# Attention chunks beside dense matmuls: one stretch per chunk, scores in quarters with the state's part, own part and update in halves

## The chip, the cores and the metric

One core of one Trainium2 chip. The metric is the device time of one execution in microseconds (us); lower is better. Stage times further down are read from a profiled execution's trace, whose span is some 2 us shorter than the device time of the same execution.

## The reference

A linear recurrence with a decay per head, for q, k, v of 4 x 8 heads x 768 steps x 64, followed by a two-layer network on its output, laid out as 3072 rows of 512.

```python
gamma = 1.0 - 2.0 ** (-5.0 - np.arange(H))
for t in range(S):                                  # S = 768, D = 64
    state = gamma * state + k[:, :, t] (outer) v[:, :, t]
    y[:, :, t] = q[:, :, t] @ state / sqrt(D)
x = y.transpose(0, 2, 1, 3).reshape(B * S, H * D)   # 3072 x 512
h = x @ w_in                                        # 512 x 2048
out = (h * sigmoid(1.702 * h)) @ w_out              # 2048 x 512
```

## The kernel before

The recurrence is computed by chunks of 128 steps: 24 chunks, six for each batch element. Matmuls run on TensorE and leave their results in PSUM tiles; SyncE's queue issues the input loads. The matmuls of the two-layer network are called dense below. A chunk goes through three steps.

- `turn`: q and k are transposed. For chunks 0 to 7 TensorE does it and ScalarE copies the result out of PSUM; for chunks 8 to 23 VectorE does it, in 32x32 squares, from tiles (`q_sq`, `k_sq`) that 16 small loads each have laid out for it.
- `attend`: the scores k·q of the chunk's eight heads into PSUM, then VectorE multiplies them with the mask of decays (`at`).
- `finish`: the part of the output that comes from the state of earlier chunks, the part from the chunk's own scores, the rescaling into X by VectorE, and the update of the state.

Four chunks make a block of 512 rows for the dense layers. Blocks 0 and 1 are multiplied plainly. From block 2 on, the up-projection takes seven products of half size in place of eight; every block's down-projection does. The steps of the next block's chunks are put between the 28 units (four matmuls, 1.73 us each) of a down-projection. So the time falls into a start-up (chunks 0 to 7 and the up-projection of block 0), the up-projection of block 1, and then for each block an output stage, with the next block's chunks in it where there are any, and the next up-projection.

```python
def turn(j, between=lambda: None):
    for name, store in (("q", QT), ("k", KT)):
        t = home(j, name + "T")
        if j < 2 * CB:                                   # CB = 4
            ...
            p = ps.tile([P, HP, P], F32, name="pt", tag="att")       # one bank, two buffers
            for hp in range(HP):
                pe.transpose(p[:, hp, :], ..., ident)
            act.activation(t, p, AF.Copy)
            between()
        else:
            tc.keep_in_program_order(dve.transpose(..., QKV.pop((name, j))...))
    ...
    if j % CB < 2 or j + 2 < 2 * CB:
        load(j + 2, "qk" if j + 2 < 2 * CB else "qkv")

def attend(j):
    p = ps_a.tile([P, 2, HP, P], F32, name="pa", tag="pa")           # two banks
    for hp in range(HP):
        for i in range(2):
            r = slice(i * D, (i + 1) * D)
            pe.matmul(p[:, i, hp, :], KT[j][r, hp, :], QT[j][r, hp, :], start=True, stop=True)
    AT[j] = home(j, "at")
    for i in range(2):
        dve.tensor_mul(AT[j][:, i], p[:, i], mask[:, i])

def finish(j):
    ...
    y = ps_a.tile([P, 2, HP, P], F32, name="py", tag="pa")           # the same two banks
    if c:                                                # state's part: 8 matmuls of 64x64
        for out, s, r in where: pe.matmul(out, old[k, s, :], qt[k, s, :], ...)
    for out, s, r in where:                              # own part: 8 of 128x64
        pe.matmul(out, vn[:, HP * r + s, :], a[:, r, s, :], ...)
    dve.tensor_mul(x[...], y[:, :, 0:2, :], rowd...)     # rescale
    ...
    u = ps.tile([P, HP, D], F32, name="pu", tag="att")   # update, in a tile of its own
    for s in range(HP):
        for r in range(2): pe.matmul(u[r * D:(r + 1) * D, s, :], kd[...], vn[...], ...)
    ...                                                  # new state = decay * old + u

# output stage of block m: one of the steps after every second unit
for n, unit in enumerate(down(m)):
    unit()
    ...
    if between and n % 2: between.pop(0)()
```

## Time and profile before

| | us |
|---|---|
| time, median of 3 runs | 713.88 (712.61 to 714.52) |
| start-up, up to the first dense matmul of 512 columns | 109.91 |
| output stage of block 1 (chunks 8 to 11 in it) | 62.61 |
| up-projection after it (no chunks) | 48.35 |
| output stages of blocks 2, 3, 4 | 62.49, 62.02, 62.62 |

In the rows of a timeline, the first two numbers are start and length in us, then the engine, the line of the program, the operation, output<-input, the tile shape of TensorE, the size of the moving operand and how many instructions the row groups. A bracket gives the idle time ahead and what ended it. L224, L245, L262, L264 and L278 are the transposes, scores, state's part, own part and update of the kernel before. Each matmul shows as two records (a transpose as one), so the 8 matmuls of the scores before are x16, the 16 quartered ones of the changed kernel x32. The granted clock is the share of its full speed at which TensorE ran.

The page's slices: busy tenths of TensorE and the granted clock in tenths, 40 slices of 17.8 us each.

```profile
PE   6799999999999999999999999999999999999997
PEclk9899999999999999999999999999999999999999
```

Apart from the last slice, TensorE has holes in the first two only, and the clock is low in the second only (0.8). TensorE's timeline of one turn in the start-up:

```profile
61.92 0.60 PE L224 MATMUL pt<-ident,q_in 128*128 128x128 f32 x4
62.36 0.60 PE L224 MATMUL pt<-ident,kn_in 128*128 128x128 f32 x4
```

The transposes of k follow those of q by 0.44 us, with no wait between. Each has a one-bank tile of its own.

### The profile page before, as it was taken

What the parts mean: (1) busy time and instruction counts of PE and PEld (TensorE: products, weight loads), DVE (VectorE), ACT (ScalarE), POOL (GpSimd) and SP (SyncE); (2) the same over time, 40 slices, a digit from 0 to 9 for tenths busy, and PEclk for the clock granted to TensorE, in tenths of its full rate; (3) what the DMA queues carried; (4) which work ended last, traced back from release to release, by engine and by line L of the source; (5) the groups of instructions that cost most, each with busy time, mean ns of one, the idle gap of its engine ahead of it and who ended that gap; (6) DMA issues with size and microseconds to landing.
All of it is one profiled execution on the core that took longest, in us unless ns stands there. A gap on an engine that the chain in (4) does not pass through costs nothing.

```text
span 710.8 us, 10300 instructions
## 1 busy us (share of the span) xinstructions
PE 692.4 (97%) x4109; PEld 572.5 (81%) x4109; DVE 363.7 (51%) x520; ACT 126.6 (18%) x197; POOL 111.5 (16%) x99
## 2 busy tenths in 40 slices
PE   6799999999999999999999999999999999999997
PEld 5688885447888888888888888888888888888886
DVE  4989889992612832443732443543345363344241
ACT  2322323311000001331000342000333000233000
POOL 2221010000564403000323000222000130200030
PEclk9899999999999999999999999999999999999999
DMA  9984443420012324101334200324300320000001
GB/s 228 290 213 116 135 147 119 135 35 8 15 46 41 74 46 104 35 0 20 74 60 102 46 0 11 75 47 88 66 1 3 72 45 24 23 1 1 15 1 44
DMA packets 143599, 46.31 MB, mean 65 GB/s; under 512 B 130752, under 2 KB 137408, under 8 KB 143552
## 3 DMA queue, kind: packets, MB, share of 16 engines
q1 hardware_dynamic: 134704, 38.84, 23.7%
q10 hardware_dynamic: 8848, 6.83, 3.1%
q8 instruction: 32, 0.52, 0.3%
q14 instruction: 15, 0.12, 0.1%
HBM read 39.33 MB, written 6.29 MB: 64 GB/s over the span
## 4 chain that ended last, share of the span: by engine, by line
PE 76%; DVE 12%; SPq 7%; issue 2%; DMA 2%; ACT 1%; DVEq 0%; ACTq 0%
PE pd L414 28%; PE px L363 16%; PE py L363 12%; PE ph L324 8%; SPq L132 6%; PE ph L311 6%; PE py L264 3%; DVE G L353 2%; PE pa L245 2%; PE py L262 2%; DVE G L354 1%; DVE G L248 1%; DVE G L352 1%; PE pu L278 1%; DMA k_sq<-in_k_dram 1%
## 5 line engine op out<-in xcount | busy, mean ns | idle before, releaser
L414 PE MATMUL pd<-W,G 128*128 128x256 f32 x1120 | 251.6, 382 | 0.4 <-DVE G L354 0.3
L414 PEld LDWEIGHTS pd<-W,G 128*128 128x128 f32 x1120 | 210.0, 190 | 31.7 <-DVE G L354 1.2
L363 PE MATMUL px<-X,W 128*128 128x256 f32 x512 | 119.0, 379 | 0.0
L363 PEld LDWEIGHTS px<-X,W 128*128 128x128 f32 x512 | 97.3, 190 | 13.2
L363 PE MATMUL py<-X,W 128*128 128x256 f32 x384 | 90.7, 379 | 0.0
L363 PEld LDWEIGHTS py<-X,W 128*128 128x128 f32 x384 | 73.0, 190 | 9.9
L311 PE MATMUL ph<-X,W 128*128 128x256 f32 x256 | 59.7, 388 | 0.0
L324 PE MATMUL ph<-W,W 128*128 128x512 f32 x128 | 55.1, 592 | 0.0
L311 PEld LDWEIGHTS ph<-X,W 128*128 128x128 f32 x256 | 48.3, 193 | 7.3 <-issue 0.2
L235 POOL TENSOR_TENSOR kd<-kn_in,cold 128x512 f32<-128x512 f32 x13 | 13.5, 1042 | 250.6 <-PE pu L278 202.0
L324 PEld LDWEIGHTS ph<-W,W 128*128 128x128 f32 x128 | 24.3, 190 | 30.2 <-issue 29.2
L355 POOL TENSOR_TENSOR G<-G 128x512 f32<-128x512 f32 x20 | 29.1, 1452 | 115.8 <-DVE G L354 113.6
L248 DVE TENSOR_TENSOR at<-pa,mask 128x512 f32<-128x512 f32 x32 | 20.6, 685 | 45.9 <-PE pa L245 45.9
L292 DVE TENSOR_TENSOR G<-G,sg 128x512 f32<-128x512 f32 x48 | 33.1, 689 | 13.7 <-ACT sg L290 13.7
L290 ACT ACTIVATE sg<-G 128x512 f32<-128x512 f32 x48 | 30.3, 631 | 51.3 <-DVE G L373 31.0
L290 ACT ACTIVATE sg<-ph 128x512 f32<-128x512 f32 x32 | 19.1, 597 | 102.3 <-PE ph L311 58.8
L414 PE MATMUL pd<-W,W 128*128 128x256 f32 x160 | 35.6, 380 | 0.4 <-DVE W L354 0.3
L414 PEld LDWEIGHTS pd<-W,W 128*128 128x128 f32 x160 | 30.2, 190 | 5.6 <-DVE W L354 1.2
L373 DVE TENSOR_TENSOR G<-py,p 128x512 f32<-128x512 f32 x16 | 11.1, 692 | 38.1 <-PE py L363 38.1
L401 ACT ACTIVATE u<-pd 128x512 f32<-128x512 f32 x6 | 3.6, 597 | 151.4 <-PE pd L414 151.4
L268 DVE TENSOR_TENSOR X<-py,rowd 128x512 f32<-128x512 f32 x20 | 13.7, 687 | 32.0 <-PE py L264 32.0
L387 DVE TENSOR_TENSOR G<-py,vv 128x512 f32<-128x512 f32 x16 | 11.1, 692 | 25.7 <-ACT vv L384 25.7
(97 smaller groups left out, 643.0 us busy)
## 6 DMA issues: line engine op xcount, KB each, us to landing
v_in<-in_v_dram SPq DMA_DIRECT2D x24, 256.0 KB, 3.9
W<-in_moe_w_in_dram SPq DMA_DIRECT2D x12, 512.0 KB, 5.2
out_dram<-o ACTq DMA_DIRECT2D x24, 256.0 KB, 2.8
W<-in_moe_w_out_dram SPq DMA_DIRECT2D x10, 512.0 KB, 3.7
q_sq<-in_q_dram SPq DMA_DIRECT2D x256, 16.0 KB, 1.8
k_sq<-in_k_dram SPq DMA_DIRECT2D x256, 16.0 KB, 1.7
kn_in<-in_k_dram SPq DMA_DIRECT2D x13, 256.0 KB, 3.3
G<-in_moe_w_out_dram SPq DMA_DIRECT2D x6, 512.0 KB, 3.6
```

The source lines that it names most:

```text
L132: tc.keep_in_program_order(sp.dma_start(t[r0:r0 + C4, hp], src[b, hp + HP * (r0 // D), rows, d0:d0 + C4].rearrange("(s p) d -> p s d", p=C4)))
L245: pe.matmul(p[:, i, hp, :], KT[j][r, hp, :], QT[j][r, hp, :], start=True, stop=True)
L248: dve.tensor_mul(AT[j][:, i], p[:, i], mask[:, i])
L262: pe.matmul(out, old[k, s, :], qt[k, s, :], start=(s < 2), stop=False, skip_group_check=True)
L264: pe.matmul(out, vn[:, HP * r + s, :], a[:, r, s, :], start=(not c and s < 2), stop=(s >= 2), skip_group_check=True)
L290: act.activation(s, h, AF.Sigmoid, scale=1.702)
L292: dve.tensor_mul(g, h[:, i], s[:, i])
L311: pe.matmul(h[:, ab], w, X[:, 2 * half + c // 2, c % 2, :], start=(ab == 0 and c == 0), stop=(c == 3), skip_group_check=True)
L324: pe.matmul(h, w, X1[:, c // 2:4:2, c % 2, :], start=(c == 0), stop=(c == 3))
L355: pool.tensor_sub(a[1], a[1], a[0])
L363: pe.matmul(acc[:, u, :], W1[:, 2 * d + u, sa, c, :], X[:, sb, c, :], start=(start and u == 0 and c == 0), stop=(stop and c == 1), skip_gr ...
L414: pe.matmul(p0[:, n, :], g1(m, p, sa)[:, n * P:(n + 1) * P], W2[:, sb, p, :], start=(new and p == 0 and n == 0), stop=(last and p == NP - ...
```

## The change

Each change of tile shape costs TensorE time (0.19 us, by the prediction's reading of the trace below). The intent is to let all of a chunk's small matmuls lie in one stretch between dense ones, with few changes of shape: the scores of chunk j+1, cut to 64x64 like the state's part of chunk j, then that state's part, then own part and update of chunk j, both of 128x64. Since the scores are a chunk ahead, the masks are ready when the own part comes. The scores and the output need separate PSUM tiles for that; the two banks come from the transposes and from the update, which move into the output's tile pair. For chunks 0 to 2 the output stays in the pair of the scores, now with the update in it. q's turned tile gets a second buffer, and loads and the decayed keys are issued later or earlier accordingly. The core of the diff:

```diff
@@ turn
-        for name, store in (("q", QT), ("k", KT)):
+        early = j < 2 * CB
+        if early:
+            p = ps_a.tile([P, 2, HP, P], F32, name="pt", tag="py")
+        for i, (name, store) in enumerate((("q", QT), ("k", KT))):
...
-                p = ps.tile([P, HP, P], F32, name="pt", tag="att")
                 for hp in range(HP):
-                    pe.transpose(p[:, hp, :], x[...], ident)
-                act.activation(t, p, AF.Copy)
+                    pe.transpose(p[:, i, hp, :], x[...], ident)
+                act.activation(t, p[:, i], AF.Copy)
                 between()
@@ attend
-    def attend(j):
+    def attend(j, f=None):
...
-            for i in range(2):
-                r = slice(i * D, (i + 1) * D)
-                pe.matmul(p[:, i, hp, :], KT[j][r, hp, :], QT[j][r, hp, :], start=True, stop=True)
+                for h in range(2):
+                    for i in range(2):
+                        r, t = slice(i * D, (i + 1) * D), slice(h * D, (h + 1) * D)
+                        pe.matmul(p[t, i, hp, :], kt[r, hp, t], qt[r, hp, :], start=True, stop=True)
+        if f is not None:
+            finish(f)
...
@@ finish
-        y = ps_a.tile([P, 2, HP, P], F32, name="py", tag="pa")
+        y = ps_a.tile([P, 2, HP, P], F32, name="py", tag="py" if j >= CB - 1 else "pa")
...
+        if c < NC - 1:
+            kd = KD.pop(j)
+            u = y[:, 0, 2:4, :]...                     # the update, in the output's tile
+            ... pe.matmul(u[...], kd[...], vn[...], start=False, ...)
         dve.tensor_mul(x[...], y[:, :, 0:2, :], rowd...)
...
-        u = ps.tile([P, HP, D], F32, name="pu", tag="att")
...
@@ order of the steps
-                for s in (lambda j=j: turn(j), lambda j=j: attend(j), lambda j=j: finish(j))]
+                for s in (lambda j=j: turn(j), lambda j=j: attend(j, j - 1))]
...
+        between, step = [], 3
+        if m == 1:
+            between = [lambda: turn(2 * CB), lambda: attend(2 * CB)] + chunks(2 * CB + 1, 3 * CB)
+            step = 2
...
-            if between and n % 2:
+            if between and n % step == step - 1:
                 between.pop(0)()
```

A step is taken after every third unit of an output stage, but after every second one in the stage of block 1, where five chunks are turned and scored in place of four (8 to 12).

More of the change, by code (lines that the diff above doesn't have):

```diff
@@ L125, in load @@
                 plain("kn", k, "k_sq", 2, True, sp if j else act)
-        else:
+        elif "q" in what:
             for name, src in (("q", q), ("k", k)):
@@ L135, in load @@
                 QKV[name, j] = t
-            if c < NC - 1:
+        if "v" in what:
+            if j >= 2 * CB and c < NC - 1:
                 plain("kn", k, "kn", 1)
-        if "v" in what:
             plain("v", v, "v", 2)
@@ L209, in home @@
         if j >= 2 * CB:
-            return one.tile([P] + shape, F32, name=name, tag=name)
+            return one.tile([P] + shape, F32, name=name, tag=name, bufs=2 - (at > 0))
         if at < 3:
@@ L216, in turn @@
     def turn(j, between=lambda: None):
-        for name, store in (("q", QT), ("k", KT)):
+        early = j < 2 * CB
+        if early:
+            p = ps_a.tile([P, 2, HP, P], F32, name="pt", tag="py")
+        for i, (name, store) in enumerate((("q", QT), ("k", KT))):
             t = home(j, name + "T")
-            if j < 2 * CB:
+            if early:
                 x = QKV["kn", j] if name == "k" else QKV.pop(("q", j))
-                p = ps.tile([P, HP, P], F32, name="pt", tag="att")
                 for hp in range(HP):
-                    pe.transpose(p[:, hp, :], x[:, 2 * hp:2 * hp + 2, :].rearrange("p i d -> p (i d)"), ident)
-                act.activation(t, p, AF.Copy)
+                    pe.transpose(p[:, i, hp, :], x[:, 2 * hp:2 * hp + 2, :].rearrange("p i d -> p (i d)"), ident)
+                act.activation(t, p[:, i], AF.Copy)
                 between()
@@ L230, in turn @@
             store[j] = t
-        if j % NC < NC - 1:
-            KD[j] = home(j, "kd")
-            x = QKV.pop(("kn", j)).rearrange("p h d -> p (h d)")
-            x = x.rearrange("p (s r d) -> p r s d", s=HP, r=2) if j < 2 * CB else x.rearrange("p (r s d) -> p r s d", r=2, s=HP)
-            pool.tensor_mul(KD[j].rearrange("p (r s) d -> p r s d", r=2), x,
-                            cold[:, H:2 * H].rearrange("p (r s) -> p r s", r=2)[:, :, :, None].to_broadcast([P, 2, HP, D]))
-        if j % CB < 2 or j + 2 < 2 * CB:
-            load(j + 2, "qk" if j + 2 < 2 * CB else "qkv")
@@ L240, in attend @@
-    def attend(j):
-        p = ps_a.tile([P, 2, HP, P], F32, name="pa", tag="pa")
-        for hp in range(HP):
-            for i in range(2):
-                r = slice(i * D, (i + 1) * D)
-                pe.matmul(p[:, i, hp, :], KT[j][r, hp, :], QT[j][r, hp, :], start=True, stop=True)
-        AT[j] = home(j, "at")
-        for i in range(2):
-            dve.tensor_mul(AT[j][:, i], p[:, i], mask[:, i])
-        KT.pop(j)
+        if early:
+            decay(j)
+        if j + 2 < NCH and (j + 2 < 2 * CB or not early):
+            load(j + 2, "qk")
@@ new lines, in decay @@
+    def decay(j):
+        if j % NC == NC - 1:
+            return
+        KD[j] = home(j, "kd")
+        x = QKV.pop(("kn", j)).rearrange("p h d -> p (h d)")
+        x = x.rearrange("p (s r d) -> p r s d", s=HP, r=2) if j < 2 * CB else x.rearrange("p (r s d) -> p r s d", r=2, s=HP)
+        pool.tensor_mul(KD[j].rearrange("p (r s) d -> p r s d", r=2), x,
+                        cold[:, H:2 * H].rearrange("p (r s) -> p r s", r=2)[:, :, :, None].to_broadcast([P, 2, HP, D]))
+    def attend(j, f=None):
+        if j is not None:
+            p = ps_a.tile([P, 2, HP, P], F32, name="pa", tag="pa")
+            kt, qt = KT.pop(j), QT[j]
+            for hp in range(HP):
+                for h in range(2):
[4 more added lines that the diff above has]
+            finish(f)
+        if j is not None:
+            AT[j] = home(j, "at")
+            for i in range(2):
+                dve.tensor_mul(AT[j][:, i], p[:, i], mask[:, i])
+            if j >= 2 * CB:
+                decay(j)
+        if f is not None and f + 2 < 2 * CB:
+            load(f + 2, "v")
+        if j is not None and 2 * CB <= j < NCH - 1:
+            load(j + 1, "v")
@@ L265, in finish @@
                       skip_group_check=True)
+        if c < NC - 1:
+            kd = KD.pop(j)
+            u = y[:, 0, 2:4, :].rearrange("p o t -> p (o t)").rearrange("p (s d) -> p s d", s=HP)
+            for s in range(HP):
+                for r in range(2):
+                    pe.matmul(u[r * D:(r + 1) * D, s, :], kd[:, HP * r + s, :], vn[:, HP * r + s, :],
+                              start=False, stop=True, skip_group_check=True)
         half, t0 = divmod(j % CB * P, TH)
@@ L269, in finish @@
                        rowd.rearrange("p (r o) t -> p r o t", r=2))
-        if j + 2 < 2 * CB:
-            load(j + 2, "v")
-        if c == NC - 1:
-            return
-        kd = KD.pop(j)
-        u = ps.tile([P, HP, D], F32, name="pu", tag="att")
-        for s in range(HP):
-            for r in range(2):
-                pe.matmul(u[r * D:(r + 1) * D, s, :], kd[:, HP * r + s, :], vn[:, HP * r + s, :],
-                          start=(s == 0), stop=True, skip_group_check=True)
         if c == 0:
             dve.tensor_copy(new, u)
-        else:
+        elif c < NC - 1:
             pool.tensor_mul(new, old, whole.rearrange("p a b -> p (a b)")[:, :, None].to_broadcast([P, HP, D]))
@@ L475, with chunks @@
                        pattern=[[0, H], [1, P]], channel_multiplier=-1)
-    def chunks(m):
-        return [s for j in range(m * CB, (m + 1) * CB)
-                for s in (lambda j=j: turn(j), lambda j=j: attend(j), lambda j=j: finish(j))]
+    def chunks(first, last):
+        return [s for j in range(first, last + 1)
+                for s in (lambda j=j: turn(j), lambda j=j: attend(j, j - 1))]
     keep_warm(7)
@@ L492 @@
                 fetch()
-        finish(j)
+        if j < CB - 1:
+            attend(None, j)
+        else:
+            attend(j + 1, j)
         if j == 0:
@@ L497 @@
             up0(0, j - 1)
-    between = chunks(1)[1:]
+    between = chunks(CB + 1, 2 * CB - 1) + [lambda: attend(None, 2 * CB - 1)]
     for n, unit in enumerate([(1, p) for p in range(3)] + [(half, p) for p in range(3, NP) for half in range(2)]):
@@ L502 @@
             narrow()
-        if between:
+        if between and n % 3 < 2:
             between.pop(0)()
@@ L511 @@
         if f >= NFF - 2:
-            load(2 * CB + f - NFF + 2)
+            load(2 * CB + f - NFF + 2, "qkv" if f == NFF - 2 else "qk")
     for m in range(NB):
-        between = chunks(m + 1) if 0 < m < NB - 1 else []
+        between, step = [], 3
+        if m == 1:
+            between = [lambda: turn(2 * CB), lambda: attend(2 * CB)] + chunks(2 * CB + 1, 3 * CB)
+            step = 2
+        elif 1 < m < NB - 2:
+            between = chunks((m + 1) * CB + 1, (m + 2) * CB)
+        elif m == NB - 2:
+            between = chunks((m + 1) * CB + 1, NCH - 1) + [lambda: attend(None, NCH - 1)]
         if m > 1:
@@ L517 @@
                 up(d)
-                if m + 1 < NB and d < 2:
-                    load((m + 1) * CB + d)
         for n, unit in enumerate(down(m)):
```

## The prediction

> **What bounds the kernel now.** I read the page's engine shares and chain first, then the order in time of TensorE, then that of the input queue. The share line and the chain of the page:
>
> ```profile
> PE 692.4 (97%) x4109; PEld 572.5 (81%) x4109; DVE 363.7 (51%) x520; ACT 126.6 (18%) x197; POOL 111.5 (16%) x99
> PE 76%; DVE 12%; SPq 7%; issue 2%; DMA 2%; ACT 1%; DVEq 0%; ACTq 0%
> ```
>
> TensorE is busy nearly all of the span and 76% of the chain; but 7% of the chain is the SyncE queue that issues the loads (SPq) and 2% its transfers. So a saving on TensorE counts in full only while that queue keeps ahead. One attention chunk of the stage that writes output block 1 (the start, the length and the group of each row of TensorE's timeline; the bracket is idle time and its releaser):
>
> ```profile
> 242.20 7.17 PE L414 MATMUL pd<-W,G 128*128 128x256 f32 x32
> 249.30 1.16 PE L245 MATMUL pa<-qT,kT 64*128 64x128 f32 x16
> 250.40 3.72 PE L414 MATMUL pd<-W,G 128*128 128x256 f32 x16
> 254.05 0.67 PE L262 MATMUL py<-qT,state 64*64 64x128 f32 x16
> 254.64 1.15 PE L264 MATMUL py<-at,v_in 128*64 128x128 f32 x16
> 255.57 0.69 PE L278 MATMUL pu<-v_in,kd 128*64 128x64 f32 x16
> 256.18 7.17 PE L414 MATMUL pd<-W,G 128*128 128x256 f32 x32
> ```
>
> A chunk is cut in two by dense work: scores (L245), 16 dense records, then state part (L262), own part (L264), update (L278). Use start to start, not the modelled ends. Dense records alone come every 216 ns (64 of them take 13.81 us, 200.28 to 214.10). The chunk lasts 256.18 - 242.20 = 13.98 us, of which 48 dense records are 48 x 0.216 = 10.36; attention therefore costs 3.62 us of TensorE, with no wait in it. Record by record inside a group, a pair of 64-row tiles comes every 112 ns, a set of four 64x64 tiles every 109 ns, a pair of 64-column tiles every 109 ns, and every 58.5 ns with 64 moving columns. Eight pairs, four sets of four, eight pairs, eight pairs: 0.89 + 0.44 + 0.87 + 0.47 = 2.67 us. The other 0.95 us are the five changes of tile shape, 0.19 each.
>
> **What the Trainium skill says.** "TensorEngine Tiling (Array Packing)", Key Properties: "Changing tiling mode (not just tile) drains the TensorE". The trace agrees: the last score record starts at 221.987, the next dense one 0.20 us later, and the one after it 0.32 later instead of 0.216. "TensorE: Matmul & The Clock Gate", Part 3, says that tiles of different row and column groups run together; the four-at-once sets above show it (109 ns for four, 109 for two). The same page, Part 1, says that an idle TensorE is throttled to half its clock until it has been busy for some 3.4 us. The trace has it in the beginning: behind a wait of 2.81 us
>
> ```profile
> 20.81 0.67 PE L262 MATMUL py<-G,state 64*64 64x128 f32 x16 [2.81 <-DVE G L248]
> 23.55 4.73 PE L311 MATMUL ph<-X,W 128*128 128x256 f32 x16
> ```
>
> 16 dense records last a microsecond longer than the 3.65 that they usually take, and the granted clock is 0.79 from 24 to 36 us. "DMA: Bandwidth & Descriptors", Issuing engines are not separate DMA queues, calls the sequencer's time to initiate a DMA "usually small relative to the DMA itself". Here it is not: q and k of a chunk take 32 issues of 0.43 us at a pace of 0.474, one behind the other, while the 16 DMA engines are only 24% to 37% busy; the issuing is what binds.
>
> **The change, part by part.**
>
> (a) Shape changes. Scores of chunk j+1 become 16 matmuls of 64x64 (32 records) right ahead of chunk j's state part, which has the same shape; own part and update are of one shape already. A stretch is now dense, quarters, halves, dense: three changes for five. Work: 8 + 4 sets of four at 109 ns = 1.31, 0.87 own, 0.47 update, together 2.65 us, against 2.67: quartering the scores gains nothing itself. With 3 x 0.19 = 0.57 a full stretch costs 3.2 us, so 0.41 less per chunk.
>
> (b) Waits on the masks. Scores used to be masked by VectorE just ahead of the own part; TensorE waited for it 0.17 to 0.25 us once per block and 0.43 and 0.45 in the start-up. Now a whole step lies between. The second PSUM tile pair (py), paid for by the two banks that transposes and update had, also lets scores start without waiting for the previous output's reading. Gain about 0.25 per block, 1 us in the start-up.
>
> (c) Start-up. Until about 45 us VectorE is 95% busy narrowing weights and sets the pace; nothing is won there, and the scores of chunk 1 now wait for the update's copy as well (some 1 us lost). Chunks 4 to 7 win 4 x 0.41 plus 1 us of waits: net -1.5.
>
> (d) Sum over stages without new waits. Block 1's output stage has one more score stretch (chunk 12's) than before: 62.6 us becomes 48.4 dense + 0.1 + 1.25 (scores of chunk 8 alone) + 3 x 3.2 + 2.75 = 62.1: -0.5. The next two: four stretches each, -1.45 and -1.4. The fourth has three full ones and a last one without scores (1.9): 62.6 to 60.0, -2.6. With -1.5: **-7.5 us**, 706.4.
>
> (e) The loads. This is where I expect the loss. The stage of block 1 now does a step after every two units of 1.73 us, and runs through five chunks' scores, not four. A chunk is due every 4 x 1.73 + 3.2 = 10.1 us (before, 14.0). The queue:
>
> ```profile
> 215.63 7.51 SPq L132 DMA_DIRECT2D q_sq<-in_q_dram  x16
> 223.24 9.10 SPq L132 DMA_DIRECT2D k_sq<-in_k_dram  x16
> 232.45 0.39 SPq L120 DMA_DIRECT2D kn_in<-in_k_dram  x1
> 232.94 0.53 SPq L120 DMA_DIRECT2D v_in<-in_v_dram  x1
> 233.56 9.66 SPq L132 DMA_DIRECT2D q_sq<-in_q_dram  x16
> 243.32 7.49 SPq L132 DMA_DIRECT2D k_sq<-in_k_dram  x16
> 250.90 0.38 SPq L120 DMA_DIRECT2D v_in<-in_v_dram  x1
> 251.39 8.83 SPq L132 DMA_DIRECT2D q_sq<-in_q_dram  x16
> 260.32 7.49 SPq L132 DMA_DIRECT2D k_sq<-in_k_dram  x16
> ```
>
> One chunk occupies it for 233.56 - 215.63 = 17.9 us, just to issue. Only chunks 8 and 9 are in before the stage; 10 can start when VectorE has turned chunk 8 over and freed its buffer:
>
> ```profile
> 214.91 0.70 DVE L228 STREAM_TRANSPOSE qT<-q_sq 128x512 f32<-128x512 f32 x1
> 215.53 0.67 DVE L228 STREAM_TRANSPOSE kT<-k_sq 128x512 f32<-128x512 f32 x1
> ```
>
> that is 1.5 us after the stage's start at 214.1. VectorE's order in the changed kernel has these two in the same place behind the last addition of block 0, so the start is the same. Loads of chunks 10, 11 and 12 then take 267.8 - 215.6 = 52.2 us, less 0.5 for a v that comes later now. q and k of chunk 12 have been issued 53.2 us into the stage, land 1.75 us later and are turned over in 2 x 0.65: ready at 56.3. TensorE wants them behind 20 units of 1.73, 1.3 for chunk 8's scores and three stretches: 34.5 + 0.1 + 1.3 + 9.6 = 45.5. **TensorE loses about 10.8 us there**, some 2.5 of it already at chunk 11 (issued at 35, ready at 38, wanted at 35.4) and the rest at chunk 12. v of chunk 10 and decayed keys (1.04 us of GpSimd) come just behind and add little. An idle time of eight microseconds also lowers the clock: +1.5, an estimate from the 1.0 and the slower small matmuls after the 2.81 us wait.
>
> Later stages hold: a chunk is due every 13.6 us against 17.9, but two are loaded ahead during the up-projection (48.4 us without chunks), so only two must arrive during a stage, at about 21 and 39 us, and they are wanted at 37 and 51. The keys of the next block's first chunk land about 58 us in; the sums of X that stand behind them in GpSimd's order are needed at about 65. No loss, with some 4 us to spare.
>
> Sum: 713.9 - 7.5 + 10.8 + 1.5 = 718.7.
>
> **The rivals.**
> 1. No starvation. If the queue got its start earlier, or issued at its bare rate (0.474 us each, 15.2 for 32), chunk 12 would be ready near 51 and 6 us would be lost; with none at all the result is 706. For it: every one of the queue's longer pauses (1.3 to 1.8 us) may depend on other traffic. Against: three chunks in a row took 17.9 us in this very stage, and the second and third blocks show 16.4 to 18.1.
> 2. More starvation: GpSimd's sums stand behind keys that come late in the third or fourth stage and stall the next up-projection: 2 to 5 us each, to 723. For it: the orders do put those keys between the sums. Against: the margins above.
> 3. The shape changes don't become cheaper, since the drain depends on what follows rather than on their number: then 7.5 falls to about 3, and the result is near 722.
> 4. VectorE's start-up chain shifts by one or two microseconds, either way.
>
> **Range and chances.** I centre a little below the sum, at 717, since rival 1 lies far to one side. 8 in 10: 706 (hardly any starvation) to 723 (rival 2 or 3). Faster by 2% needs 699.6, below even the case without new waits: 0.02. Slower by 2% needs 728: 0.04.
>
> **What would show it.** (a) Right if a full stretch takes 3.1 to 3.3 us beyond its dense records; wrong at 3.5 and more. (b) Right if no wait on the masked scores is left after 50 us. (e) Right if TensorE has an idle time of 5 to 9 us ahead of scores in block 1's stage, released by VectorE's turning of k, which itself waited for a k load; the queue would be unbroken through that stage. The other three stages should be 1.4 to 2.6 us shorter than before. The prediction is wrong if that idle time is missing, or if a wait of that size appears ahead of an up-projection.

## The result

| | before | changed |
|---|---|---|
| time, median of 4 runs | 714.2 (712.61 to 714.88) | 722.84 (721.8 to 724.79) |
| mean clock, profiled run | 0.995 | 0.986 |
| span, profiled run | 710.8 | 721.3 |

The ratio is 1.0127, with a 95% interval of 1.0099 to 1.0155: the changed kernel is slower by 1.3%, less than the 2% of the classes but clear of the noise. A ratio here is the mean time of one kernel's fast runs over that of the other's of the same rounds, so not quite the ratio of the medians.

By stages of the two traces:

| stage | before | changed | difference | expected |
|---|---|---|---|---|
| start-up | 109.91 | 117.17 | +7.26 | -1.5 |
| output of block 1 | 62.61 | 72.06 | +9.45 | +11.8 (-0.5 + 10.8 + 1.5) |
| up-projection after it | 48.35 | 48.35 | 0 | 0 |
| output of block 2 | 62.49 | 60.74 | -1.75 | -1.45 |
| output of block 3 | 62.02 | 60.27 | -1.75 | -1.4 |
| output of block 4 | 62.62 | 59.84 | -2.78 | -2.6 |
| sum | | | +10.4 | +4.9 |

The sum agrees with the spans (721.3 - 710.8 = 10.5). One expectation in this table has the wrong sign, the first.

The page after: engine shares, the chain's shares, and the slices (18.0 us each).

```profile
PE 689.9 (96%) x4493; PEld 574.2 (80%) x4493; DVE 360.3 (50%) x520; ACT 127.3 (18%) x197; POOL 110.8 (15%) x99
PE 86%; DVE 6%; SPq 3%; ACT 2%; DMA 2%; issue 1%; DVEq 0%; ACTq 0%
...
PE   5889899999999987999999999999999999999997
PEclk9699999999999998999999999999999999999999
```

TensorE is busy 2.5 us less than before although it has 384 more instructions. The holes are at two places: in the first three slices and the fifth, and in the 15th and 16th (252 to 288 us). The clock drops to 0.6 in the second slice and to 0.8 in the 16th. The chain's share of the input queue has become smaller, 3% after 7%, so the average says nothing of the queue's harm, which lies in one stage. An ordinary stretch, in the stage of block 2 (L258, L283, L285 and L293 are scores, state's part, own part and update):

```profile
354.79 10.63 PE L433 MATMUL pd<-W,G 128*128 128x256 f32 x48
365.34 1.10 PE L258 MATMUL pa<-qT,kT 64*64 64x128 f32 x32
366.27 0.62 PE L283 MATMUL py<-qT,state 64*64 64x128 f32 x16
366.81 1.14 PE L285 MATMUL py<-at,v_in 128*64 128x128 f32 x16
367.74 0.68 PE L293 MATMUL py<-v_in,kd 128*64 128x64 f32 x16
368.35 10.63 PE L433 MATMUL pd<-W,G 128*128 128x256 f32 x48
```

From 354.79 to 368.35 are 13.56 us; 48 dense records take 48 x 0.216 = 10.36; the stretch costs 3.20, where before the same work cost 3.62. No bracket is left. This part is as intended. The stage of block 1 isn't; TensorE's timeline there, from the scores of chunk 10 on:

```profile
248.03 1.10 PE L258 MATMUL pa<-qT,kT 64*64 64x128 f32 x32 [1.36 <-DVE kT L230]
...
275.38 1.98 PE L258 MATMUL pa<-qT,kT 64*64 64x128 f32 x32 [6.56 <-DVE kT L230]
277.11 1.10 PE L283 MATMUL py<-qT,state 64*64 64x128 f32 x16
278.14 1.42 PE L285 MATMUL py<-at,v_in 128*64 128x128 f32 x16
279.50 14.08 PE L433 MATMUL pd<-W,G 128*128 128x256 f32 x64
```

The scores of chunk 10 wait 1.36 us; a row left out, the own part of chunk 10, waits 0.42 us for the load of v. The scores of chunk 12 wait 6.56 us for VectorE's turning of k. Behind the wait the small matmuls are slow: scores 277.11 - 275.38 = 1.73 us in place of 0.92, state's part 1.03 in place of 0.54, own part 1.36 in place of 1.07; together 1.6 us. The granted clock was 0.50 from 272 to 278 us. VectorE's row ahead of it, and the input queue's issues of that stage:

```profile
274.52 0.71 DVE L230 STREAM_TRANSPOSE kT<-k_sq 128x512 f32<-128x512 f32 x1 [4.90 <-DMA k_sq<-in_k_dram]
```

```profile
222.89 8.67 SPq L132 DMA_DIRECT2D q_sq<-in_q_dram  x16
231.66 7.73 SPq L132 DMA_DIRECT2D k_sq<-in_k_dram  x16
...
265.55 7.49 SPq L132 DMA_DIRECT2D k_sq<-in_k_dram  x16
```

Between these rows the queue is never idle for more than a tenth of a microsecond: three chunks take 273.04 - 222.89 = 50.2 us just to issue. VectorE waits for its loads, TensorE for VectorE.

What had not been foreseen is in the start-up. The turn of chunk 5, and the row of the transposes in the view of waits (engine, line, releaser: us in total, times, longest):

```profile
57.06 0.60 PE L226 MATMUL pt<-ident,q_in 128*128 128x128 f32 x4
59.41 0.66 PE L226 MATMUL pt<-ident,kn_in 128*128 128x128 f32 x4 [1.75 <-ACT G L227]
```

```profile
PE pt L226 <- ACT G L227: 9.9, 8, 2.7
```

The transposes of k now wait for ScalarE in each of the eight early chunks, 9.9 us in all. L227 is the copy of q's transposes out of PSUM. Before, there was no wait on ScalarE ahead of a transpose. (The 22.1 us in the first expectation below add the weight loads' waits for the same copies, 12.2 us; that is largely the same time counted twice.) VectorE, which the prediction took to set the pace here, was busy for 29.0 of the first 45 us, after 33.5 before the change.

### The profile page after: what moved, and what is told of

It reads as the page before. It is cut to its first block, busy times and chain, and to the rows that moved or that the text cites. A ratio compares the mean times of both kernels' runs of the same rounds, so it can differ in the third digit from the quotient of the medians.

```text
span 721.3 us, 11040 instructions
## 1 busy us (share of the span) xinstructions
PE 689.9 (96%) x4493; PEld 574.2 (80%) x4493; DVE 360.3 (50%) x520; ACT 127.3 (18%) x197; POOL 110.8 (15%) x99
## 4 chain that ended last, share of the span: by engine, by line
PE 86%; DVE 6%; SPq 3%; ACT 2%; DMA 2%; issue 1%; DVEq 0%; ACTq 0%
PE pd L433 35%; PE px L382 15%; PE py L382 11%; PE ph L343 8%; PE ph L330 7%; SPq L132 3%; PE py L285 3%; PE pa L258 3%; PE py L283 1%; PE py L293 1%; ACT W L188 1%; PE pt L226 1%; ACT G L227 1%; DVE W L372 1%; DVE G L372 1%
## 5 line engine op out<-in xcount | busy, mean ns | idle before, releaser
L433 PE MATMUL pd<-W,G 128*128 128x256 f32 x1120 | 247.6, 381 | 0.4 <-DVE G L373 0.3
L258 PE MATMUL pa<-qT,kT 64*64 64x128 f32 x512 | 18.5, 285 | 7.9 <-DVE kT L230 7.9
L424 DVE TENSOR_TENSOR o<-pd,vv 128x512 f32<-128x512 f32 x12 | 7.7, 686 | 35.9 <-ACT vv L420 35.9
```

Of the source, the lines that this page charges most:

```text
L258: pe.matmul(p[t, i, hp, :], kt[r, hp, t], qt[r, hp, :], start=True, stop=True)
L433: pe.matmul(p0[:, n, :], g1(m, p, sa)[:, n * P:(n + 1) * P], W2[:, sb, p, :], start=(new and p == 0 and n == 0), stop=(last and p == NP - ...
```

## The experiments

Three theories stood for the start-up: (T) the transposes of q and k share one PSUM tile, so those of k wait until q's half has been copied; (U) the update lies in the output's tile, so the rescaling waits for the update's matmuls and, in chunks 0 to 2, the next scores, which use the same pair, wait for the copy of the state; (V) nothing of both: VectorE's chain of narrowing weights shifted, or it is chance. For the stage of block 1: (Q) one queue's issuing is too slow for five chunks; (B) the transfers themselves are; (P) only the pace of the steps matters.

The start-up depends on chance as well, so each kernel's start-up time is split at the first run of 32 dense records. The part behind it repeats within 0.05 us for one kernel.

### The kernels as they are, once more

The kernel before twice, the changed one once, unedited, to learn how much a start-up varies.

> The kernel before, once more with a profile, to see how far chance moves its start-up: 109.9 us in the one profile so far; 109 to 112 expected. All later stages as before to 0.2 us.

> The kernel before a third time, for the same reason: start-up 109 to 112 us, all later stages as before to 0.2 us.

> The changed kernel once more with a profile: start-up 115.5 to 119.5 us, as in its own profile (117.2) and the two variants that share its start-up (119.4 and 115.4); block 1's stage 71.5 to 73.

| | time, us | start-up | of it behind the first 32 dense | stage of block 1 |
|---|---|---|---|---|
| before (first trace) | 712.85 | 109.91 | 65.53 | 62.61 |
| before_again | 713.96 | 111.06 | 65.54 | 62.62 |
| before_third | 712.94 | 109.57 | 65.53 | 62.62 |
| changed (first trace) | 723.16 | 117.17 | 67.12 | 72.06 |
| after_again | 722.29 | 115.85 | 67.12 | 72.07 |

The stage of block 1 and the second part of the start-up repeat; the first part moves by 1.5 us in these traces. The runs e3 and e5 below, whose start-up code is that of the changed kernel, reach the split at 52.26 and 48.26 us, so its first part moves by 4.0. The clock goes with it: up to the split the mean granted clock was 0.86 and 0.87 in the changed kernel's first trace (split at 50.05) and e3, and 0.93 in after_again (48.73) and e5. Still, the kernel before needs 109.6 to 111.1 us and the changed start-up 115.4 to 119.4 in all its traces, so chance (V) is not the account of the loss. In the changed kernel the scores of chunk 4 lie ahead of the split and in the kernel before behind it, 1.1 us in the trace; a comparison between these two kinds has to allow for that.

### e1_own_banks: a PSUM tile for each of q and k

```diff
-            p = ps_a.tile([P, 2, HP, P], F32, name="pt", tag="py")
...
+                p = ps.tile([P, HP, P], F32, name="pt", tag="xy"[i])
-                    pe.transpose(p[:, i, hp, :], x[...], ident)
-                act.activation(t, p[:, i], AF.Copy)
+                    pe.transpose(p[:, hp, :], x[...], ident)
+                act.activation(t, p, AF.Copy)
```

> The changed kernel, with the transposes of q and of k in two tiles of one PSUM bank each (taken from the banks of the up-projection's outputs) and not in the two halves of one tile. Theory A (k's transposes of a chunk wait until ScalarE has read q's, since both stand in one tile; the 22.1 us of waits for ScalarE's copy in the changed kernel's start-up come from this): those waits go, the start-up (first dense matmul of 512 columns at 117.2 us; before the change 109.9) comes to 110 to 112, and the time falls from 722.8 to 716 to 718. Rival B (the start-up is lost since scores wait for the state update that now stands in the output's tile, and by VectorE's order): the waits move there, start-up stays at 115 to 117, time 721 to 723.

Measured: 720.02 us, ratio to before 1.0085 (1.0062 to 1.0107). Start-up 113.35, of it behind the split 63.51 in place of 67.12. The time was expected at 716 to 718 and the start-up at 110 to 112; the gain was smaller. The turn of chunk 5, and the dense row behind the turn of chunk 6:

```profile
56.85 0.60 PE L225 MATMUL pt<-ident,q_in 128*128 128x128 f32 x4
57.29 0.60 PE L225 MATMUL pt<-ident,kn_in 128*128 128x128 f32 x4
...
73.10 3.72 PE L329 MATMUL ph<-X,W 128*128 128x256 f32 x16 [0.77 <-DVE W L310]
```

k follows q by 0.44 us again, as before the change. The waits that went away behind the split are 1.75, 0.79 and 1.80 us (chunks 5, 6 and 7 of the changed kernel), 4.3 together; 0.77 came back as a wait for VectorE, and 3.6 remain. That supports T, with a size. Ahead of the split no transpose waits for ScalarE either, but the scores of chunks 0 and 4 then do (2.42 and 0.81 us), and this part is no shorter than the scatter allows (49.84). The stage of block 1, where no such transposes are, took 73.06 us here, and 73.0 to 73.1 in e2 and e6 as well, in place of 72.06. In e1 the microsecond lies in the waits for loads: 7.08 in place of 6.56 at chunk 12 and 0.75 in place of 0.42 for v, with a slower own part behind them.

### e2_one_copy: one shared tile, but one copy after all eight transposes

```diff
-                act.activation(t, p[:, i], AF.Copy)
-                between()
+                if i:
+                    both = G[:, 0:2, j % 2 * 2:j % 2 * 2 + 2].rearrange("p a s t -> p a (s t)")
+                    act.activation(both, p.rearrange("p a b c -> p a (b c)"), AF.Copy)
+                    between()
+                    between()
```

> The changed kernel with its one tile for both transposes kept, but one ScalarE copy for both halves behind all eight transposes, so that none of them waits for a copy. Theory A: as with two tiles, start-up at 110 to 113, since a copy of 1024 columns takes some 1.1 us and only the first five chunks' scores wait for it directly; time 716 to 719. Rival B: no change, 721 to 723.

Measured: 716.92 us, ratio 1.0039 (1.0016 to 1.0062). Start-up 112.58, behind the split 62.59 (a wait of 0.19 us cuts the first run of 32 in two here; its start is taken). The turn of chunk 5:

```profile
57.46 0.60 PE L226 MATMUL pt<-ident,q_in 128*128 128x128 f32 x4
57.90 0.60 PE L226 MATMUL pt<-ident,kn_in 128*128 128x128 f32 x4
```

The tile is still shared and no second tile is used; only the reading between q and k is gone, and with it the loss. So the number and place of the banks didn't cost the time; what did is that TensorE had to wait with one half of a tile until ScalarE had read the other. In time it is 3.1 us ahead of e1; 0.9 of that is behind the split in the profile. The rest was not followed up: the profiled run of e2 is the slowest of its four (719.63), and e1's first part of the start-up (49.84 and 49.99 for e2) gives none of it.

### e3_pace: the ten steps of block 1's stage spread over 26 units, not 20

```diff
-            if between and n % step == step - 1:
+            if between and (n in (1, 3, 6, 9, 11, 14, 17, 20, 23, 25) if m == 1 else n % step == step - 1):
```

> The changed kernel with the ten attention steps of block 1's output stage spread over 26 of its 28 units and not over 20, so that each chunk is wanted after its loads. Theory C (that stage waits for the load queue, which needs 17 us a chunk to issue): its length falls from 72.1 us to 62 to 63.5, the 6.6 us of idle time ahead of chunk 12's scores goes to under 0.7, and the time falls by 8.5 to 10 to 713 to 714.5. Rival D (the loads would come later too, since each load is issued behind the step that frees its buffer): the idle time stays above 3 us, time 717 to 722. The sums of X then stand closer to the next up-projection, which must show no wait for them.

Measured: 715.57 us, ratio 1.003 (1.0004 to 1.0055); the stage of block 1 took 62.70 us in place of 72.06. Start-up 119.40, with the shared tile still there (67.14 behind the split). The scores of chunk 12:

```profile
280.18 1.10 PE L258 MATMUL pa<-qT,kT 64*64 64x128 f32 x32
```

They start without any wait; those of chunk 10 still wait 0.69 us, and the up-projection behind gets a new wait, 1.10 us for a copy by ScalarE (e9 shows the like). That stage took 49.68 in place of 48.35. With the slower pace the wait for loads at chunk 12 is gone, but this doesn't tell Q from B: both have more time.

### e4_banks_pace: e1 and e3 together

The edit is that of e1 and that of e3.

> Both edits together. If A and C are both right and independent, the gains add: 722.8 - 5 to 7 - 8.5 to 10 = 706 to 709, which beats the kernel before by some 1%. If only C is right, 713 to 714; if the start-up's gain is lost in a later wait, 712 or more.

Measured: 709.86 us, ratio 0.995 (0.9932 to 0.9969), start-up 111.32, stage of block 1 62.71, up-projection behind it 49.53. Each stage shows the gain of its own repair. Both repairs together are worth 722.84 - 709.86 = 13.0 us, where alone they gave 2.8 and 7.3; the 2.9 us above the sum were not taken apart, but the traces differ in two more places: e1's longer waits for loads (1.0) are gone, and the first part of the start-up took 47.81 us after 49.84 in e1, at a mean granted clock of 0.93 after 0.86. The result is faster than the kernel before.

### e5_k_on_act: ScalarE's queue issues the k loads of chunks 10 to 12

```diff
-                        tc.keep_in_program_order(sp.dma_start(
+                        tc.keep_in_program_order((act if name == "k" and CB * 2 + 2 <= j <= CB * 3 else sp).dma_start(
```

> The changed kernel with its fast pace kept, but the k loads of chunks 10, 11 and 12 issued on ScalarE's queue beside the q loads on SyncE's. Same bytes, same pieces, same DMA engines. Theory C1 (the stage of block 1 is bound by the time one queue takes to issue, 0.474 us each): chunk 12 is ready before it is wanted, the stage falls from 72.1 us to 62 to 64, time 713 to 715. Rival D1 (bound by the DMA engines or the memory, not by issuing): the two queues share the same engines, each load lands later, the stage stays above 68 us, time 719 or more.

Measured: 713.75 us, ratio 0.9999 (0.9977 to 1.0021). The pace is that of the changed kernel, the bytes are the same; the stage of block 1 took 63.38 us. TensorE's scores of chunks 10 and 12, then the issues of both queues:

```profile
246.25 1.10 PE L258 MATMUL pa<-qT,kT 64*64 64x128 f32 x32 [1.37 <-DVE kT L230]
...
266.48 1.10 PE L258 MATMUL pa<-qT,kT 64*64 64x128 f32 x32
```

```profile
221.10 18.33 SPq L132 DMA_DIRECT2D q_sq<-in_q_dram  x32
...
245.54 8.54 SPq L132 DMA_DIRECT2D q_sq<-in_q_dram  x16
```

```profile
221.74 9.36 ACTq L132 DMA_DIRECT2D k_sq<-in_k_dram  x16
231.38 8.41 ACTq L132 DMA_DIRECT2D k_sq<-in_k_dram  x16
```

q and k of a chunk are issued side by side, and the queues now have pauses: none issues a load from 241.4 to 245.5 us. The waits at chunk 12 and for v are gone, and so are 8.7 us of this stage; the up-projection behind took 48.88 in place of 48.35, with a wait of 0.29 us for ScalarE's copy. This decides between Q and B in favour of Q: the same transfers, issued by two queues, are in time. It also speaks against P as the whole account, since the pace is unchanged. The 1.37 us at chunk 10 stayed although its loads came in half the time, so that part isn't the queue's: VectorE turns chunk 10 over directly behind six additions (239.7 to 244.8 us), with no wait for a load.

### e6_u_apart: e1, and for chunks 0 to 2 the rescaling first and the update in a tile of its own

```diff
(the edit of e1, and:)
+        def rescale(): ...                             # the tensor_mul into X, as before
+        if j < CB - 1:
+            rescale()
+            kd = KD.pop(j)
+            u = ps.tile([P, HP, D], F32, name="pu", tag="xy"[j % 2])
+            for s in range(HP):
+                for r in range(2):
+                    pe.matmul(u[r * D:(r + 1) * D, s, :], kd[:, HP * r + s, :], vn[:, HP * r + s, :],
+                              start=(s == 0), stop=True, skip_group_check=True)
+        elif c < NC - 1:
...
-        dve.tensor_mul(x[...], y[:, :, 0:2, :], rowd...)
+        if j >= CB - 1:
+            rescale()
```

> The run with transposes in two banks (start-up 113.4 us, time 720.0), and besides the update of the state of chunks 0 to 2 in a bank of its own again, behind the rescaling of the output as before the change. Theory B (what is left of the start-up's loss, 3.4 us in that run, comes from the update standing in the output's tile: the rescaling waits for the update's matmuls, the next scores for VectorE's copy of the state, and TensorE's clock falls in these waits): the first dense matmuls of 256 columns begin at 23.5 to 24.5 us and not at 29.0, the start-up comes to 107.5 to 109.5 (before the change 109.9), time 714 to 716.5. Rival: the loss is VectorE's order alone or chance in the first loads; the start-up stays at 112 or more, time 718 to 721.

Measured: 717.24 us, ratio 1.0045 (1.002 to 1.0071), start-up 111.12, behind the split 63.51 as e1; 107.5 to 109.5 and 714 to 716.5 were expected. The scores of chunk 1 in TensorE's timeline of e6:

```profile
16.22 1.10 PE L257 MATMUL pa<-G 64*64 64x128 f32 x32 [0.41 <-DVE X L289]
```

In the changed kernel these scores wait 1.81 us, released by VectorE's copy of the state; here 0.41, released by the rescaling. The first dense matmuls start at 25.70 (before 23.55, changed 28.56). All three kernels with the update apart have start-ups of 110.0 to 111.1, mean 110.6, the two with only the tiles separated (e1, e4) 113.35 and 111.32, mean 112.3. So U is worth about 1.7 us. That is within the scatter of one start-up; it is the difference of means, and the wait in the trace, that carry it. So do the first dense matmuls: they start between 24.36 and 25.70 us in these three kernels, and between 27.57 and 30.53 in the seven traces with the update in the output's tile. Part of the 1.7 us is a low clock: e1 has a mean of 0.86 up to the split, and at the same 0.93 the split comes at 47.81 us in e4 and at 47.08 and 46.49 in e8 and e9.

### e7_quarters_alone: the kernel before, with only the scores quartered

```diff
-            for i in range(2):
-                r = slice(i * D, (i + 1) * D)
-                pe.matmul(p[:, i, hp, :], KT[j][r, hp, :], QT[j][r, hp, :], start=True, stop=True)
+            for h in range(2):
+                for i in range(2):
+                    r, t = slice(i * D, (i + 1) * D), slice(h * D, (h + 1) * D)
+                    pe.matmul(p[t, i, hp, :], KT[j][r, hp, t], QT[j][r, hp, :], start=True, stop=True)
```

> The kernel before the change with nothing but its scores cut into quarters of 64x64 (16 matmuls for 8). The prediction said that this gains nothing itself: scores stay at 1.09 us a chunk, time within 0.5 of 713.9. The changed kernel's trace has them at 1.03 where they stand alone, so the rival is a gain of 0.06 x 24 = 1.4 us: 712.5.

Measured: 713.75 us, ratio 0.9996 (0.9972 to 1.002): no change in time. In the trace the scores with their change of shape take 1.034 us in place of 1.092, and the four stages with chunks are 0.17 to 0.18 us shorter each, while the start-up behind the split takes 0.34 longer (65.87). The time can't separate no gain from the rival's 1.4 us. Twice as many instructions of half the size neither cost nor win anything that a time would show. The gain of the stretches is that of their order.

### e8_apart_act: e6 and e5 together

The edit is that of e6 and that of e5.

> All three: transposes in two banks, early updates apart, k loads of chunks 10 to 12 on ScalarE's queue. If the three causes are independent: start-up 107.5 to 109.5, block 1's stage 62 to 64, time 704.5 to 707, which is faster than the kernel before by some 1.1%; above 710 would mean that one gain is lost in another wait.

Measured: 709.31 us, ratio 0.9943 (0.9915 to 0.997). Start-up 110.59, stage of block 1 63.38, up-projection 48.35. All three causes are taken away, and the mean clock is 0.995 again. The expectation, 704.5 to 707 with a start-up of 107.5 to 109.5, was missed: the stage of block 1 came as expected, the start-up didn't, and what (c) hoped to win there is not seen.

### e9_best: e8, with block 1's steps a unit later from the scores of chunk 10 on

```diff
-            if between and n % step == step - 1:
+            if between and (n in (1, 3, 5, 7, 9, 12, 14, 16, 18, 20) if m == 1 else n % step == step - 1):
```

> The best of the runs so far (transposes in two banks, early updates apart, k loads of chunks 10 to 12 also on ScalarE's queue), with the steps of block 1's output stage one unit later from chunk 10's scores on. In the run without this the stage took 63.4 us, with 1.43 us of waiting ahead of chunk 10's scores, since VectorE turns chunk 10 over behind six additions that wait for TensorE. Expected: that wait goes, the stage takes 61.9 to 62.2 us, the start-up 110 to 112, time 707 to 709. If the wait only moves along, 63 us and 709 to 710.

Measured in five rounds: 707.91 us (705.92 to 710.01) against 714.5 of the kernel before; ratio 0.9909 (0.9888 to 0.993). It beats both kernels. The stage of block 1 took 61.94 us, without a wait; the wait at chunk 10 was one of pace, and is gone: VectorE's turn of chunk 10, behind the same six additions, is now done before TensorE wants it. The up-projection behind took 50.39 in place of 48.35. Its first rows on TensorE, ScalarE's output stores of that time and ScalarE's copy:

```profile
281.57 1.97 PE L393 MATMUL px<-X,W 128*128 128x256 f32 x8 [1.80 <-ACT p L400]
```

```profile
274.11 6.62 ACTq L436 DMA_DIRECT2D out_dram<-o  x3
280.83 0.60 ACT L400 ACTIVATE p<-px 128x512 f32<-128x512 f32 x1 [10.73 <-DMA k_sq<-in_k_dram]
```

ScalarE's sequencer is occupied with issuing three stores until 280.73, and does its copy directly behind. TensorE waits 1.80 us for that copy. (The bracket of the copy names a load, but the copy comes 0.1 us behind the last issue.) So in its trace e9 gives back 2.04 where it wins 1.44 in block 1's stage, and the intervals of e8 and e9 overlap: that e9 is ahead of e8 isn't shown, only that both are ahead of the kernel before. A wait for the same copy was there in e3.

## Why the prediction was right or wrong

The time fell into the range, at its upper end: 722.84 for 706 to 723. That was luck: the upper end was kept for rivals 2 and 3, neither of which came, and the loss that carried the time there, the start-up's, stood in no rival at this size. The change itself was told badly: +3.1 expected (717 against 713.9), +8.6 measured.

- **(a), shape changes: right.** A full stretch costs 3.20 us, as worked out. That quartering alone gains nothing held as well (e7: 0.06 us per chunk in the trace, nothing in time).
- **(b), waits on the masks: right.** No wait on a mask is left after 50 us.
- **(c), start-up: wrong, and it is the step that failed.** It said "net -1.5"; it measured +7.3 in the first pair of traces. The means of all traces are 110.2 for the kernel before and 117.0 for those with the shared tile (changed, e3, e5, after_again), +6.8. I had read the move of transposes and update into the output's banks only for what it frees ("paid for by the two banks that transposes and update had"), and had not asked who reads those tiles and who waits for the reading. The runs showed in its place: the shared tile of the transposes, 3.6 us behind the split, where the traces repeat (4.6 by the means of the whole start-up, 117.0 less 112.3 of e1 and e4, but the last microsecond lies in the scatter of the first part), and the update in the output's tile, about 1.7. Of (c)'s "the scores of chunk 1 now wait for the update's copy as well (some 1 us lost)" the mechanism was right, and its size was not far off. (The 95% that (c) gives for VectorE holds from 12 to 48 us.) What it said of chunks 4 to 7 (4 x 0.41 + 1) came only in part: behind the split, e1 takes 63.51 and the kernel before 65.53 - 1.1 = 64.4, some 0.9 gained. The kernel before waited 0.88 us for masks there and e1 does not; the stretches give some 0.8 (chunk 4's scores lie ahead of the split); and 0.77 is lost again to a wait for VectorE's weights, where the kernel before has none.
- **(d), the later stages: right.** -1.75, -1.75 and -2.78 for -1.45, -1.4 and -2.6.
- **(e), the loads: right in mechanism, somewhat too large.** The stage would be 62.1 us without waits and took 72.06: 10.0 lost, where 10.8 + 1.5 = 12.3 were expected. The traces split it into 6.56 at chunk 12, 1.36 at chunk 10, 0.42 for v, and 1.6 for the lower clock. The queue needed 50.2 us for three chunks, not 52.2. The 2.5 us at chunk 11 didn't come; instead chunk 10 waited, and not for loads but for VectorE's additions ahead of its turn: e5 halved the loads' time and it stayed, e9 moved the step and it went.
- **The rivals.** 1 (no starvation) fell. 2 (a stalled up-projection in a later block) did not come in the changed kernel, and 3 (shape changes not cheaper) fell. 4 came nearest to the start-up's fault, but put it down to VectorE's chain and at one or two microseconds.

In sum, the start-up missed by 8.8 us one way, and (d) and (e) by 0.8 and 2.3 the other way: 4.9 expected by the steps, 10.4 in the traces. The centre of 717 then stood another 1.7 below the sum, for the sake of rival 1.

Left open: what makes the first microseconds vary (44.04 to 45.52 us to the split in three traces of the kernel before, 48.26 to 52.26 in four of the changed start-up). In the four, the lower clock goes with the later split; whether it is the cause or the result of other waits was not tested. And how much of e2's lead over e1 is real.

## What to carry to other kernels

Before moving two outputs into one PSUM tile, list who reads each half and who writes next: halves in different banks still waited for each other here, and two tiles of one bank each did the same work without a wait. When a change lets a stage consume its inputs faster, divide the queue's issuing time per chunk into the new interval; where it doesn't fit, a second issuing queue or a slower pace costs little, as long as the next stage doesn't then wait for the engine that issues. And a stage by stage sum must include the stage in which "nothing is won", since the same edit can lose there.

## What the Trainium skill lacked or had wrong

- "Perfetto Trace Analysis", Optimizing Tensor Performance, Matmuls, advises to rotate independent matmul groups through different PSUM banks so that evacuation overlaps the next group. That was not enough here: q's and k's transposes lay in different banks, but in one tile, and waited 9.9 us in eight waits for ScalarE's reading. With a tile for each, no transpose waited for ScalarE, and the part of the start-up that repeats was 3.6 us shorter. The page lacks the word that in a program like this one, where waits are set per tile, the groups need tiles of their own.
- "DMA: Bandwidth & Descriptors", Issuing engines are not separate DMA queues, says that issuing from several engines only saves the sequencer's time, "usually small relative to the DMA itself". With 16 small loads for a tile that time was the bound: 50.2 us for three chunks on one queue; with k on a second one the stage fell from 72.06 to 63.38 us. That section has no sign by which to know it; "Perfetto Trace Analysis", What "DMA-bound" means, has one (the issuing engine's track is solid), and the queue's rows here agree, with pauses of 0.1 us between them.
- "TensorEngine Tiling (Array Packing)", Key Properties, says that a change of mode drains TensorE and gives no cost. The runs fit some 0.2 us each: two changes fewer took a chunk from 3.62 to 3.20 us, and 0.06 of that came with quartered scores alone (e7).
- "TensorE: Matmul & The Clock Gate", Part 1, has an idle TensorE run at half its clock. The traces agree behind the wait of 6.56 us: the granted clock was 0.50 from 272 to 278 us. They add what that cost in small matmuls: 1.6 us, with scores of 1.73 us in place of 0.92. In the start-ups the clock was low behind shorter waits too (before the change 0.61 and 0.53 from 32 to 36 us, behind one of 1.77 us); what brought it down there was not tested.
